# Attention and a state-space convolution in one kernel: half of x and all parameters transposed by DMA, zeroing by DMA, later bulk loads, and the accumulator copies on VectorE

## The chip, the core and the metric

The kernel runs on one core of one Trainium2 chip. The metric is the device time of one execution in microseconds, as the median of several executions. A profile is one further execution with the hardware profiler on; its times are counted from the first instruction, and its "span" is the time from the first instruction to the last.

## The reference

Two branches read the same input x (2048 rows of 448 numbers, bf16) and are mixed row by row with a gate g:

```python
x = A_x
g = _sigmoid((x * gate_w).sum(-1, keepdims=True))
a = _A_ref(x, A_wq, A_wk, A_wv, A_wo)
b = _B_ref(x, B_A_re, B_A_im, B_B_re, B_B_im, B_C_re, B_C_im, B_log_dt, B_Dskip)
return g * a + (1 - g) * b
```

Branch a is attention with 16 query heads of width 28 that share one key head and one value head:

```python
q = (lambda x, *d: x.transpose(*d))((x @ wq).reshape(B, S, H, Dh), 0, 2, 1, 3)
k = x @ wk
v = x @ wv
scores = jnp.einsum("bhqd,bkd->bhqk", q, k) * (Dh ** -0.5)
p = _softmax(scores, axis=-1)
o = jnp.einsum("bhqk,bkd->bhqd", p, v)
return (lambda x, *d: x.transpose(*d))(o, 0, 2, 1, 3).reshape(B, S, H * Dh) @ wo
```

Branch b is a causal convolution of every column of x with its own kernel of 2048 taps, plus x times Dskip. The taps come from 256 complex modes per column:

```python
logdA = dt * A
dB = dt * Bc
P = jnp.exp(logdA[:, :, None] * l[None, None, :])
K = jnp.einsum("dn,dnl,dn->dl", Cc, P, dB).real
```

The convolution is written with an FFT in the reference; the kernel computes it directly with matrix products.

## The kernel before

**Attention.** The work is cut into 16 blocks. Block i takes the 512 query rows of chunk i // 4 and the four heads of group i % 4. A block has 64 score tiles (16 key tiles by 4 heads) of 128 keys by 512 queries. Tiles are taken in sets of three and two in turn. For each set, TensorE computes the scores (L1181, "qk") into PSUM psS, ScalarE takes the exp of the whole set in one instruction (L1205) into a ring of 15 slots, expT, and TensorE multiplies four tiles at a time by the values (L1214, "PV") and adds into one PSUM bank, psB, called bank 6. One column of the values is 1, so the sum of the exps comes out in the same bank.

At the end of a block, `norm(i)` copies bank 6 to SBUF (the accumulator copy). Only then can the first PV of the next block overwrite the bank. The copy is ScalarE's for blocks 0 to 13 (L1074), VectorE's for block 14 (L1076), and the last block has an ending of its own. After the copy, GpSimd's queue carries three small DMAs that bring the sums into another layout and back (denT, R_scratch, rdenB), and VectorE multiplies by the reciprocal (L1088). Four blocks of one chunk then give the output rows (`outp`, `fold`).

Before block i + 2 the queries for it are projected (`qproj`): four matmuls (L816), a VectorE maximum of the magnitudes (L822), one matmul that subtracts a bound of the scores (L825), and a VectorE copy to bf16 (L828). The bound uses `kap`, the maximum over all keys, so no block can start before all four quarters of x have become keys.

**Convolution branch.** For groups of 32 columns, VectorE makes powers of the modes (`masters`) and tables of them (`tables`, L895 to L935). TensorE turns the tables into taps (`kgen`, L959), ScalarE evicts them (L972), and DMAs write them to a scratch tensor in HBM and read them back with shifted rows (T). TensorE then multiplies T by U, a layout of x with its rows in blocks of 64 (`conv`, L1015), VectorE scales (L1026), TensorE turns the result (L1037), and VectorE adds it into O (L1045), the output tile in SBUF. O and the padded rows of Wo must be zero before the first additions and products.

**The head.** Everything before the first exp of attention. x is loaded in four quarters of 512 rows (`loads`, xst). For each quarter (`prep_x`) TensorE transposes 16 squares (L565), ScalarE (L574) and VectorE (L576) each copy half of it to xT, TensorE makes the keys (L582), ScalarE evicts them (L588), and VectorE takes the maximum (L591). The columns of x are cut into four pieces of 112. In between, `prep_params` makes the seeds of the modes out of the six parameter tensors (448 x 256 each). Each is loaded with columns first (raw), transposed by TensorE (`trans`, L739), and multiplied on VectorE (L750, L753, L754, L756); ScalarE takes two sines (L757, L758) and two exps (L762, L764). VectorE also clears tiles (L450): U, Wq, Wk, Wo and O.

**What sets the order.** Nothing is ordered by hand. Every operation is recorded with an estimate of its length (ns), the keys it reads and writes, and a priority pr. The class `Prog` then plans: at each step it takes, over all engines, the operation that could start earliest, and among equals the one with the lower pr. It plans five queues: TensorE (pe), ScalarE (act), VectorE (dve), GpSimd (pool) and SP, which issues nearly all loads. Each engine carries out its planned list strictly in order, and waits on semaphores where the plan has a dependence. A DMA's planned cost comes from its row count and row size (`dma`, L140). A key that is read by one operation and written by a later one makes the later one wait for the earlier one's end, DMAs included. `fill` adds matmuls with a zero operand (L636, L640, L1187) where TensorE would have little to do.

The accumulator copy and the rule for the next PV in the code before:

```python
if i < 14:
    pg.op("act", lambda e: e.activation(av, self.psB.v(0, P, 0, [[1, 512]]), AF.Copy), 490, rd=[("b", 6)], wr=[ak, kb], pr=-1)
elif i == 14:
    pg.op("dve", lambda e: e.tensor_copy(av, self.psB.v(0, P, 0, [[1, 512]])), el(512), rd=[("b", 6)], wr=[ak, kb], pr=0)
...
o = pg.op("pe", mm, 230, rd=["va"] + [("e", t % RING) for t in ts], wr=[("b", 6)], pr=0.5, mode="c", st=4.54)
```

Of the kernel before, what the change touches and what calls it, by code (L numbers as in the profile page):

```python
# [11 lines left out]
P = 128  # L12
# [19 lines left out]
HALVES = (13,)  # L32
NTR = 5
# [47 lines left out]
class Prog:  # L81
# [52 lines left out]
    def dma(self, pairs, desc, slot, rd=(), wr=(), pr=0, eng="sp", slow=False, extra=0):  # L134
        kw = dict(allow_slow_non_contiguous=True) if slow else {}

        def fn(e):
            return [e.dma_start(o, i, **kw) for o, i in pairs]  # L138
        nd, size = desc
        o = self.op(eng, fn, nd * (30.0 + 0.03 * size if size < 1500 else 105.0 + 0.022 * size) / 16.0 * 1.1, rd, wr, pr)  # L140
        o.slot, o.ndma, o.extra = slot, len(pairs), extra
        prev = self.slots.get(slot)
        if prev is not None:
            o.deps[prev] = 1
        self.slots[slot] = o.i
        return o
# [210 lines left out]
class Kernel:  # L357
# [18 lines left out]
    def build(self):  # L376
        nc = self.nc
        with self.es:
# [5 lines left out]
            self.prep_params()  # L384
            self.prep_gate()
# [6 lines left out]
    def alloc(self):  # L392
# [26 lines left out]
        self.tslots = [(self.T, s * TW, ["tpdone", "rawdone"]) for s in range(NTR)]  # L419
# [26 lines left out]
    def consts(self):  # L446
# [13 lines left out]
        dm(self.Wq.v(0, P, 28, [[32, 64], [1, 4]]), 0.0, 300, ["Wq"])  # L460
# [22 lines left out]
        dm(V(self.Wo, 0, NT * D), 0.0, 810, ["Wo"], 5)  # L483
        for q in range(4):
            dm(V(self.O, q * 4 * D, 4 * D), 0.0, 800, [("O", q)], 5)

    def loads(self):
# [4 lines left out]
        def lx(q):  # L492
            pg.dma([(self.xst.v(0, P, q * 4 * D, [[1, 4 * D]]), dram(x, q * 4 * P * D, [[4 * D, P], [1, 4 * D]]))],
                   (128, 3584), f"x{q}", wr=[("xst", q)])
# [4 lines left out]
        def lraw(k):  # L499
            pg.dma([(raw.v(0, DT, k * 1024, [[1, 1024]]), dram(ins[names[k]], 0, [[1024, DT], [1, 1024]]))],  # L500
                   (112, 2048), f"raw{k}", wr=[("raw", k)])
# [3 lines left out]
        pg.dma([(self.dtb.v(0, P, 0, [[1, D]]), dram(ins["B_log_dt"], 0, [[0, P], [1, D]]))], (128, 896), "ldt", wr=["dt"], eng="act")  # L505
        lx(0)
        lraw(0)
        for k, (w, n) in enumerate((("A_wk", DH), ("A_wv", DH), ("gate_w", 1))):
            pg.dma([(wks.v(0, DT, 112 * k, [[n, 4], [1, n]]), dram(ins[w], 0, [[n, DT], [DT * n, 4], [1, n]]))],
                   (448, 2 * n), f"wk{k}", wr=[("wks", k)], eng="act", slow=True)  # L510
        for q in range(1, 4):
            lx(q)
        pg.dma([(wst.v(0, DT, 0, [[D, 4], [1, D]]), dram(ins["A_wq"], 0, [[D, DT], [DT * D, 4], [1, D]]))],
               (448, 896), "wq", wr=["wqs"])
        lraw(1)
        pg.op("dve", lambda e: e.tensor_copy(self.Wk.v(0, DT, 0, [[32, 16], [1, DH]]),
                                             wks.v(0, DT, 0, [[DH, 4], [0, 4], [1, DH]])), 300, rd=[("wks", 0)], wr=["Wk"], pr=-0.6)
        pg.op("dve", lambda e: e.tensor_copy(self.Wq.v(0, DT, 0, [[32, 64], [1, DH]]),
                                             wst.v(0, DT, 0, [[DH, 64], [1, DH]])), 620, rd=["wqs"], wr=["Wq"], pr=-0.5)
        pg.op("dve", lambda e: e.tensor_copy(self.Wv.v(0, DT, 0, [[32, 4], [1, DH]]), wks.v(0, DT, 112, [[DH, 4], [1, DH]])),  # L520
              180, rd=[("wks", 1)], wr=["Wv"], pr=0.1)
        pg.op("dve", lambda e: e.tensor_copy(self.Wv.v(0, DT, 28, [[32, 4]]), wks.v(0, DT, 224, [[1, 4]])),
              100, rd=[("wks", 2)], wr=["Wvg"], pr=0.1)
        rs = self.U.rs
        for k, (h, p0, b0) in enumerate(((1, 16, 15), (0, 0, 15), (1, 0, 31))):
            ap = bass.AP(tensor=self.U.h, offset=h * rs + p0 * D, ap=[[2 * rs, 64], [D, 16], [1, D]])
            pg.dma([(ap, dram(x, 64 * b0 * D, [[D, 64], [-64 * D, 16], [1, D]]))],
                   (1024, 896), f"u{k}", rd=["Uz"] if p0 else [], wr=[("U", k)], pr=0.5)
        for k in range(2, 6):
            lraw(k)  # L530
        pg.dma([(self.skt.v(32 * g + 31, 1, 0, [[8, 14], [1, 8]]), dram(ins["B_Dskip"], 8 * g, [[16 * D, 1], [32, 14], [1, 8]]))
                for g in range(4)], (112, 8), "sk", rd=["skt"], wr=["skt"], pr=1, slow=True)
        w = ins["A_wo"]
        pg.dma([(self.Wo.v(32 * r, DH, 0, [[D, 4], [1, D]]), dram(w, DH * r * D, [[D, DH], [4 * DH * D, 4], [1, D]]))
                for r in range(4)], (448, 896), "wo", rd=["Wo"], wr=["Wo"], pr=2)
        pg.dma([(dram(self.KP, KH + 1024, [[4 * KW, 112], [KW, 4], [1, 64]]), self.kstg.v(0, 112, 0, [[64, 4], [1, 64]]))],
               (448, 128), "pad", rd=[("kst", 0, 0), ("kst", 1, 0)], wr=["pad"], pr=3)
# [15 lines left out]
    def prep_x(self):  # L553
        pg = self.pg
        xst, xT, kT = self.xst, self.xT, self.kT
        sm = self.small
        for q in range(4):
            for hp in range(2):
# [3 lines left out]
                def mm(e, q=q, hp=hp, t=t, o=o):  # L562
                    for Tl in range(2):
                        for k in range(4):
                            r = e.matmul(t.v(0, DT, o + 512 * Tl + 128 * k, [[1, 128]]),  # L565
                                         xst.v(0, P, (4 * q + k) * D + (2 * hp + Tl) * DT, [[1, DT]]),
# [733 lines left out]
```

## Time and profile before

| What | Value |
|---|---|
| Median of three executions | 541.87 us (540.47 to 544.5) |
| The profiled execution | 540.75 us, span 539.0 us |
| ScalarE busy | 497.5 us (92%) |
| TensorE matmuls busy, fillers included | 486.4 us (90%) |
| VectorE busy | 449.5 us (83%) |
| GpSimd busy | 102.1 us (19%) |
| Exps of attention (L1205), 410 instructions | 470.6 us |
| Accumulator copies on ScalarE (L1074) | 14 |
| First exp of attention starts | 26.74 us |
| Last exp of attention ends | 527.7 us |

A row of the profile's order of time reads: start in us, length in us, engine, line of the kernel, operation, what it writes and reads with sizes, how many instructions the row merges, and in brackets how long the engine had been idle before it and what ended that. In the table of stages, each engine has its busy time and number of instructions within the stretch; PEclk is the clock granted to TensorE as a share of full speed. The chain of waits is followed back from the last instruction: at each step to what released it, or to the instruction before it on its engine.

### The profile page before, as it was taken

How to read it: one execution, taken by the hardware profiler on the slowest of the kernel's cores; microseconds unless marked ns; L12 is line 12 of the kernel's file. 1: busy time of each engine (PE TensorE's matmuls, PEld its weight loads, DVE VectorE, ACT ScalarE, POOL GpSimd, SP SyncE). 2: the span in 40 equal slices, each digit the busy share in tenths (PEclk: the TensorE clock that was granted, in tenths of full speed). 3: DMA queues.
4: the chain of work that ended last, by engine and by line, in shares of the span. 5: the costliest groups of instructions: out<-in, count | busy, mean ns of one | idle time of the engine just before them, and what ended most of it. 6: DMA issues, size and time to landing. Idle time of an engine off the chain costs nothing.

```text
span 539.0 us, 20180 instructions
## 1 busy us (share of the span) xinstructions
PE 486.4 (90%) x9186; PEld 249.5 (46%) x9186; DVE 449.5 (83%) x891; ACT 497.5 (92%) x458; POOL 102.1 (19%) x192
## 2 busy tenths in 40 slices
PE   7698999989999899888999898989999898999887
PEld 4442233235454555353555454553556355644434
DVE  7979999989999999899999999999999695331203
ACT  3799999998999999989999999999999796899992
POOL 2000002200431404012040430040042213220000
PEclk9989999998999999999999999999999796899998
DMA  8931100793398987979778989999859997999722
GB/s 235 283 121 47 37 21 7 251 347 116 118 376 300 329 358 284 351 259 386 296 240 363 327 273 348 400 351 367 343 191 356 353 380 287 348 344 392 261 88 71
DMA packets 39042, 142.89 MB, mean 265 GB/s; under 512 B 11240, under 2 KB 22032, under 8 KB 24620
## 3 DMA queue, kind: packets, MB, share of 16 engines
q1 hardware_dynamic: 28316, 135.30, 69.0%
q0 software_dynamic: 9104, 6.13, 4.4%
q8 instruction: 72, 1.18, 0.9%
q10 hardware_dynamic: 1536, 0.17, 0.3%
q14 instruction: 14, 0.11, 0.1%
HBM read 135.39 MB, written 5.74 MB: 262 GB/s over the span
## 4 chain that ended last, share of the span: by engine, by line
ACT 56%; PE 26%; DMA 8%; DVE 8%; issue 2%; ACTq 0%
ACT expT L1205 54%; PE psS L1181 7%; PE psB L1214 4%; PE psS L959 3%; PE psX L959 3%; DMA rdenB<-R_scratch 3%; PE psX L1015 3%; DMA denT<-acc 2%; DMA sz<-in_A_wv_dram 2%; PE psS L1015 2%; ACT acc L1074 1%; DMA R_scratch<-denT 1%; DVE msq L856 1%; DVE xT L576 1%; DVE tab L911 1%
## 5 line engine op out<-in xcount | busy, mean ns | idle before, releaser
L1205 ACT ACTIVATE expT<-psS 128x1536 bf16<-128x1536 f32 (+1 forms) x410 | 470.6, 1340 | 18.7 <-PE psS L1181 11.7
L1181 PE MATMUL psS<-qT,kT 32*128 32x512 bf16 x1024 | 164.3, 395 | 29.8 <-ACT expT L1205 22.3
L1214 PE MATMUL psB<-expT,vaug 128*32 128x512 bf16 x1024 | 105.1, 400 | 3.7 <-issue 3.2
L1181 PEld LDWEIGHTS psS<-qT,kT 32*128 32x128 bf16 x1024 | 39.5, 91 | 119.3 <-ACT expT L1205 97.3
L1187 PE MATMUL psB<-ident,zero 32*128 32x512 bf16 x190 | 74.9, 394 | 0.0
L911 DVE TENSOR_TENSOR tab<-tab,mbf 128x256 bf16<-128x256 bf16 (+5 forms) x75 | 69.6, 928 | 1.2
L1015 PE MATMUL psX<-T,U 128*18 128x128 bf16 (+7 forms) x1920 | 54.7, 243 | 4.2 <-issue 3.2
L1214 PEld LDWEIGHTS psB<-expT,vaug 128*32 128x32 bf16 x1024 | 26.4, 93 | 64.8 <-issue 62.8
L1015 PEld LDWEIGHTS psX<-T,U 128*18 128x18 bf16 (+7 forms) x1920 | 47.6, 161 | 15.1 <-issue 11.2
L640 PE MATMUL psB<-ident,zero 128*32 128x512 bf16 (+3 forms) x728 | 48.6, 336 | 0.0
L138 POOL DMA_DIRECT2D KP_scratch<-xT x64 | 34.4, 544 | 43.6 <-ACT xT L972 43.6
L138 POOL DMA_DIRECT2D KP_scratch<-kstg x63 | 34.1, 549 | 34.2 <-ACT kstg L972 32.5
L959 PE MATMUL psX<-tab 128*32 128x64 bf16 x960 | 39.7, 293 | 0.3 <-DVE tab L935 0.3
L913 DVE TENSOR_TENSOR tmp<-tab,mbf 128x256 bf16<-128x256 bf16 (+4 forms) x62 | 39.6, 638 | 0.0
L1015 PE MATMUL psS<-T,U 128*32 128x128 bf16 (+7 forms) x1344 | 39.3, 243 | 0.0
L138 POOL DMA_DIRECT2D denT<-acc x15 | 10.8, 717 | 146.8 <-ACT acc L1074 137.9
L1015 PEld LDWEIGHTS psS<-T,U 128*32 128x32 bf16 (+7 forms) x1344 | 34.0, 161 | 8.9 <-issue 6.9
L959 PE MATMUL psS<-tab 128*32 128x64 bf16 x832 | 35.3, 293 | 0.0
L138 POOL DMA_DIRECT2D R_scratch<-denT x15 | 8.6, 576 | 138.7 <-DVE denT L1082 59.2
L930 DVE TENSOR_TENSOR tab<-tab,tmp 128x2048 bf16<-128x2048 bf16 x28 | 33.5, 1219 | 0.2
L959 PEld LDWEIGHTS psX<-tab 128*32 128x32 bf16 x960 | 30.3, 138 | 6.7 <-issue 3.8
L959 PEld LDWEIGHTS psS<-tab 128*32 128x32 bf16 x832 | 26.4, 137 | 7.4 <-issue 5.4
(179 smaller groups left out, 599.1 us busy)
## 6 DMA issues: line engine op xcount, KB each, us to landing
T<-KP_scratch SPq DMA_DIRECT2D x102, 1072.0 KB, 11.0
xT<-KP_scratch SPq DMA_DIRECT2D x7, 1072.0 KB, 10.5
rdenB<-R_scratch POOLq DMA_DIRECT2D x15, 256.0 KB, 12.4
tab<-KP_scratch SPq DMA_DIRECT2D x3, 1072.0 KB, 8.8
U<-in_A_x_dram SPq DMA_DIRECT2D x3, 896.0 KB, 15.4
tab<-in_A_x_dram SPq DMA_DIRECT2D x4, 448.0 KB, 7.5
SZ_scratch<-tab SPq DMA_DIRECT2D x1, 1344.0 KB, 8.6
out_dram<-O SPq DMA_DIRECT2D x3, 448.0 KB, 3.8
```

Source lines behind the costliest of these rows:

```text
L138: return [e.dma_start(o, i, **kw) for o, i in pairs]
L576: pg.op("dve", lambda e, d=dst, s=src: e.tensor_copy(d, s), 1130, rd=[("b", b)], wr=[key], pr=-0.6)
L640: r = e.matmul(t.v(32 * j, 32, bo, [[1, 128 * m]]), self.zero.v(0, P, 0, [[1, 32]]), self.ident.v(0, P, 0, [[0, m], [1, P]]), start=not ac ...
L911: vo(lambda e, dst=dst, src=src, mr=mr: e.tensor_tensor(dst, src, mr, ALU.mult), 2 * n, done + mk(lv), kr + ki)
L913: vo(lambda e, src=src, mi=mi, w=w, n=n, tb=tb, to=to: e.tensor_tensor(tb.v(0, P, to, [[n, 2], [cw, w], [1, cw]]), src, mi, ALU.mult), 2 * ...
L930: vo(lambda e, h=h: e.tensor_tensor(tab.v(0, P, FM + 32 * h, [[64, 2], [EW, 32], [1, 32]]), tab.v(0, P, lo + 31 * EW + 64 * h, [[BLK, 2], ...
L959: r = e.matmul(G.v(32 * g, 32, 64 * jj, [[1, 64]]), tab.v(0, P, lo + comp * BLK + 32 + o, [[EW, 32]]), tab.v(0, P, fo, [[mo - fo, 2], [EW, ...
L1015: r = e.matmul(ps.v(32 * j, 32 - 2 * n, 128 * k, [[1, 128]]), self.U.v(0, P, 2 * n * D + 4 * gi + j, [[D, 32 - 2 * n]]), tb.v(0, P, to + j ...
L1181: r = e.matmul(self.psS.v(0, P, 512 * (bo + k), [[1, 512]]), kT.v(32 * h, 32, 128 * kt, [[1, 128]]), qT.v(32 * h, 32, 512 * (i % 2), [[1, ...
L1187: r = e.matmul(self.psB.v(0, P, 0, [[1, 512]]), self.zero.v(32 * h, 32, 0, [[1, P]]), self.ident.v(32 * h, 32, 0, [[0, 4], [1, P]]), start ...
L1205: pg.op("act", lambda e: e.activation(expT.v(0, P, 512 * es, [[1, n]]), self.psS.v(0, P, 512 * bo, [[1, n]]), AF.Exp, scale=SQ), 50 + n / ...
L1214: r = e.matmul(self.psB.v(32 * h, 32, 0, [[1, 512]]), vaug.v(0, P, 32 * kt, [[1, 32]]), expT.v(0, P, 512 * (t % RING), [[1, 512]]), start= ...
```

## The change

It has these parts.

- The accumulator copies of blocks 0 to 13 are made by VectorE (pr 0) instead of ScalarE (pr -1).
- Quarters 0 and 1 of x are transposed by DMA straight into xT; quarters 2 and 3 go the old way and come first. The four column pieces are now 128 wide (the fourth starts at column 320 and overlaps the third by 64 columns; the weights of the overlap are zero), so the copies of Wk, Wq, Wv and the gate's weights are split and get zeroed rows.
- The six parameter tensors are transposed by DMA; TensorE's transposes of them are gone, and the VectorE products read SBUF.
- Wo and O are zeroed by five DMAs from a zero tile, not by VectorE. These DMAs name ("mb", 10) as read, so the first writing of that key, the last level of the first `masters`, waits for them.
- The U, Dskip, Wo and pad transfers are recorded later (`late`), and Dskip and pad also wait for the seeds ("sqq"). The loads of the head get an order of their own (DP).
- wq is loaded in two pieces, the first with head group 0. The projections of the values are recorded tile by tile with a lower pr.
- The seeds of the first group are copied by VectorE instead of two DMAs. The last level of `masters` is written straight into the bf16 table.
- The planner's cost of a DMA row is lower for short rows.

The core of the diff:

```diff
+DP = dict(x2=-1.00, x3=-0.95, raw0=-0.90, x0=-0.85, raw1=-0.80, wq0=-0.75, x1=-0.70, wq1=-0.65)
...
-        o = self.op(eng, fn, nd * (30.0 + 0.03 * size if size < 1500 else 105.0 + 0.022 * size) / 16.0 * 1.1, rd, wr, pr)
+        o = self.op(eng, fn, nd * (12.0 + 0.036 * size if size < 1500 else 105.0 + 0.022 * size) / 16.0 * 1.1, rd, wr, pr)
...
+    def tdma(self, pairs, ns, slot, wr, pr):
+        o = self.dma(pairs, (1, 1), slot, (), wr, pr)
+        o.fn = lambda e: [e.dma_start_transpose(a, b) for a, b in pairs]
+        o.ns = ns
         return o
...
-        dm(V(self.Wo, 0, NT * D), 0.0, 810, ["Wo"], 5)
-        for q in range(4):
-            dm(V(self.O, q * 4 * D, 4 * D), 0.0, 800, [("O", q)], 5)
...
+            pg.tdma([(self.xT.v(0, P, 2048 * q, [[512, 3], [1, 512]]), dram(x, 512 * q * D, [[D, 512], [1, 384]])),
+                     (self.xT.v(0, P, 2048 * q + 1536, [[512, 1], [1, 512]]), dram(x, 512 * q * D + D - P, [[D, 512], [1, P]]))],
+                    2900, f"x{q}", wr=self.xk(q), pr=DP[f"x{q}"])
...
-            pg.dma([(raw.v(0, DT, k * 1024, [[1, 1024]]), dram(ins[names[k]], 0, [[1024, DT], [1, 1024]]))],
-                   (112, 2048), f"raw{k}", wr=[("raw", k)])
+            pg.tdma([(raw.v(0, P, k * 1024, [[D, 2], [1, D]]), dram(ins[names[k]], 0, [[NM, D], [1, NM]]))],
+                    1270, f"raw{k}", wr=[("raw", k)], pr=DP.get(f"raw{k}", 0))
...
-        for q in range(4):
-            for hp in range(2):
+        for q in (2, 3, 0, 1):
+            for hp in range(2) if q > 1 else ():
...
-        p0, k0 = trans(0, -0.4)
-        vt(tt(1), p0, dtp2, ALU.mult, [k0, "rd"], [K(1)], -0.4, unlock=p0)
+        vt(t(1), rw(0), dtp2, ALU.mult, [("raw", 0), "rd"], [K(1)], -0.65)
...
+    def late(self):
...
+        for k, (h, p0, b0) in enumerate(((1, 16, 15), (0, 0, 15), (1, 0, 31))):
...
+        for k, (b, n, keys, pr) in enumerate(((self.Wo, 14, ["Wo"], 1.9), *((Sub(self.O, 4 * D * q), 14, [("O", q)], 5 + q) for q in range(4)))):
+            pg.dma([(b.v(0, P, 0, [[P, n], [1, P]]), self.zero.v(0, P, 0, [[0, n], [1, P]]))], (P * n, 256), f"z{k}", rd=["zero", ("mb", 10)], wr=keys, pr=pr)
...
+            pg.op("dve", lambda e: e.tensor_copy(self.sz.v(0, P, 0, [[BW, 3], [1, w]]), self.seed.v(0, P, o, [[W2, 3], [1, w]])), 270,
+                  rd=["sz0", "sz1", "sq"], wr=["sre", "sim", "sqq"] + [("wks", k) for k in range(3)], pr=0.9)
...
+                if k == 10:
+                    dv(lambda e: e.scalar_tensor_tensor(last(1), f[0], 2.0, f[1], ALU.mult, ALU.mult), w, keys(9) + tp, [("mb", 10)])
+                    dv(lambda e: e.tensor_tensor(last(0), f[2], f[3], ALU.subtract), w, ["msq"] + tp, [("mb", 10)])
+                    continue
...
-        if i < 14:
+        if i < 0:
             pg.op("act", lambda e: e.activation(av, self.psB.v(0, P, 0, [[1, 512]]), AF.Copy), 490, rd=[("b", 6)], wr=[ak, kb], pr=-1)
-        elif i == 14:
+        elif i < 15:
             pg.op("dve", lambda e: e.tensor_copy(av, self.psB.v(0, P, 0, [[1, 512]])), el(512), rd=[("b", 6)], wr=[ak, kb], pr=0)
```

## The prediction, made before the result was known

> **What bounds the kernel now.** I first read the stages: the span was cut where the chain of waits and the order of time change character, and the busy time of each engine was taken in each cut. The cuts are: before the first exp, the first crowded stretch, the long body, the last stretch with convolution work, exps alone, and the end.
>
> ```profile
> core 0: us, PE busy (x) PEld busy (x) DVE busy (x) ACT busy (x) POOL busy (x), PEclk, DMA share, GB/s
> 0.00:26.74 26.74, 18.70 (x188) 11.29 (x188) 23.09 (x41) 14.79 (x16) 3.44 (x20) 0.97 0.94 261
> 26.74:42.50 15.76, 15.18 (x153) 6.12 (x156) 11.73 (x18) 13.99 (x13) 0.00 (x0) 0.84 0.30 104
> 42.50:420.00 377.50, 346.12 (x6915) 174.71 (x6907) 365.87 (x725) 369.96 (x339) 82.03 (x144) 0.99 0.74 268
> 420.00:471.50 51.50, 47.55 (x901) 27.59 (x901) 32.16 (x76) 41.51 (x39) 10.23 (x19) 0.80 0.94 341
> 471.50:527.70 56.20, 50.99 (x1002) 24.84 (x998) 12.06 (x23) 56.20 (x51) 6.44 (x11) 1.00 0.76 270
> 527.70:539.00 11.30, 7.88 (x40) 4.96 (x40) 4.62 (x11) 1.11 (x3) 0.00 (x0) 0.85 0.13 42
> ```
>
> ScalarE is the bound from 42.5 us on: 370.0 of 377.5 us busy, and 56.2 of 56.2 in the last stretch of exps. Only in 420 to 471.5 us does it idle for 10 us; there the granted clock is 0.80. VectorE is 97% busy in the body but 21% busy in the last 56 us, so its own total does not set the end. The first 26.7 us hold no attention exp at all.
>
> Next I read ScalarE's order of time around an accumulator copy, and the one block (the fifteenth) whose copy is already VectorE's.
>
> ```profile
> 59.55 0.78 ACT L1074 ACTIVATE acc<-psB 128x512 f32<-128x512 f32 x1
> 60.02 28.34 ACT L1205 ACTIVATE expT<-psS 128x1024 bf16<-128x1024 f32 x25
> ...
> 151.81 0.60 ACT L1074 ACTIVATE acc<-psB 128x512 f32<-128x512 f32 x1
> 152.30 4.64 ACT L1205 ACTIVATE expT<-psS 128x1536 bf16<-128x1536 f32 x4
> ```
>
> ```profile
> 499.71 0.69 DVE L1076 COPY acc<-psB 128x512 f32<-128x512 f32 x1 [2.83 <-PE psX L1015]
> ```
>
> A copy lasts 0.60 us, but the next exp begins 0.47 to 0.49 us after it began: 0.49 is what it takes from the exps. VectorE's copy is 0.69 us, and the exps around it run without a gap; but VectorE was idle there.
>
> Last, the chain of waits before the first exp, in order of time.
>
> ```profile
> 1.73 10.10 DMA sz<-in_A_wv_dram
> ...
> 14.17 1.14 DVE xT L576
> 15.31 1.00 DVE T L756
> 16.31 0.09 DVE expT L522
> 16.39 0.12 issue
> 16.51 0.81 DVE O L450
> 17.32 1.08 DVE xT L576
> 18.40 0.59 DVE small L591
> 18.98 1.13 DVE xT L576
> 20.11 0.53 DVE Wq L518
> 20.65 0.59 DVE small L591
> 21.24 1.00 DVE T L750
> ```
>
> From 11.8 to 24.8 us that chain is VectorE, almost without a break. Clearing O (0.81 us, and once more at 22.45) and the x copies (some 1.1 us each) stand in it. So VectorE's load sets the head, not arriving data.
>
> **What the Trainium skill says.** "ScalarE: Activation LUTs", section "What ACT_TABLE_LOAD costs", gives an ACTIVATE with immediates 186 ns + 0.833 N and an overlap of 93 ns between neighbours: 613 ns for 512 columns, 520 ns of stream. The trace agrees with the first (597 median) and has 0.47 to 0.50 for the second; I use 0.49. "VectorE: DVE Perf Modes", section "Why PSUM operands drop a tier", holds an fp32 PSUM source to the 1x rate; the 0.69 us above agrees, and in the chain such an instruction advances VectorE by 0.60. For a DMA transpose the trace has no row. "DMA: Bandwidth & Descriptors", section "Latency and other measured facts", has 261 GB/s for one with a non-contiguous middle dimension; the planner's costs in the diff (2.9 us for a quarter of x, 1.27 us for a parameter) are slower, 181 GB/s with the 64 columns of x that are read twice.
>
> **The change part by part.**
>
> *Accumulator copies.* 14 copies leave ScalarE. Twelve lie in the body, where it idles 2% of the time: 12 x 0.49 = 5.9 us gained. Two lie in 420 to 471.5 us, where TensorE at the lower clock holds the exps back anyway: 0 to 1.0 us. I take 6.0. VectorE gets 14 x 0.60 = 8.4 us. The new wait is TensorE's: the next block's first PV needs the accumulator bank, and behind that PV in TensorE's order stand the next scores, which ScalarE needs. The copy queues behind what VectorE has in hand, at most 2.28 us (the 4096-column products of L911 and L913), often 0.3 to 0.7. On ScalarE it also queued, behind an exp of 1.1 us. Bounds: nothing at all, and 1.4 us of idle ScalarE per boundary (priced below). I take nothing, because the planner orders scores ahead of that PV and one set of scores already in PSUM feeds ScalarE for another 1.1 us.
>
> *Head, VectorE.* Needed there before the first exp after the change: dt and its scaling 0.7, Wk 0.4, Wq for the first head group 0.3, the phase chain 1.08+0.62+1.08+1.08 = 3.9, two x copies 2.4, four key maxima 2.7, the second parameter 1.1, Wv and gate 0.5, kap and Wb 0.4, first q 1.4: 13.8 us. Starting at 7.2 us, as L729 does now, that gives 21.0 us. Gone from the stretch are two x copies (2.4) and two clears of O (1.6); three more clears stood before it.
>
> *Head, data.* SP now sends x2, x3, raw0, x0, raw1, wq0, x1 in this order. Today's first quarter of x is issued at 0.81 and used at 6.36: 5.5 us, of which 448 KB at the 283 GB/s of the page's second slice are 1.6, so 3.9 us are latency and company. Plain bytes ahead of x1's end (two quarters, a part of wq, small weights: 1.18 MB) take 4.2 us; the transposes by the planner's costs 2 x 2.9 + 2 x 1.27 = 8.3 us. Landing: 0.8 + 3.9 + 4.2 + 8.3 = 17.2 us. From there follow, by today's rows, the key projection 1.04, its eviction 0.69, the maximum 0.67, kap and Wb 0.41, L825 0.50, the q copy 0.69, the first scores 0.66 and some 0.5 of hand-overs: 5.2 us. First exp at **22.4 us** instead of 26.74, so 4.3 us gained. At the skill's 261 GB/s the data would be 2.6 us earlier (5.7 us instead of 8.3, an estimate from that page), and VectorE's 21.0 plus the last QK then decides, some 21.7. At half the planner's rate x1 lands at 25.5 and the first exp stands at 30.7, a loss of 4.0.
>
> *TensorE and ScalarE in the head.* 32 transposes of x and 48 of the parameters go (some 1.5 and 3.4 us of TensorE), two ScalarE x copies of 1.02. All stand beside VectorE's chain or x1's arrival: nothing more than counted. The parameter products keep their 1.08 us, reading SBUF instead of PSUM.
>
> *Zeroing by DMA, loads later.* 5 x 0.81 = 4.0 us leave VectorE, 1.6 counted above. Five DMAs of 1792 rows of 256 bytes come on SP. The U loads with 1024 rows kept SP for 10.10/3 = 3.4 us each; by rows that makes 5.9 us each, 29 us in all. Behind them wait Dskip, Wo, pad, the seed stores and the gate's round trip: SP is free near 50 us instead of 29. The first kernel taps are evicted at about 90 us, so this is hidden. One wait is new: the last level of the first masters writes what the zeroing names as read, so VectorE waits there for all five to land, about 53 us. That level stands at 59 us today: hidden, with little to spare.
>
> *Masters and seeds.* The last level is written straight into its table: 3 x 0.42 + 0.29 and 3 x 0.29 + 0.22 = 2.6 us less VectorE; two seed copies replace two DMAs, 0.6 more; the split weight copies and clears 0.9 more. VectorE's sum: +8.4 - 4.0 - 2.4 - 2.6 + 0.6 + 0.9 = +0.9 us. Since the last 56 us leave it 44 us idle: nothing.
>
> *Sum.* -6.0 - 4.3 = -10.3; I give back 0.3 for clears and copies that move into the crowded stretch after the first exp. 539.0 - 10.0 = 529.0 us of span. The profiled execution was 540.75 us and the median of three 541.87, so the prediction on the median is **531.9 us**.
>
> **The rivals.** (A) *Slow transposes.* At half the planner's rate the head costs 4.0 instead of giving 4.3: 541.87 - 6.0 + 4.0 = 539.9, no change. For it: no transposing DMA in the trace. Against it: two sources above the halved rate. (B) *Absorbed.* ScalarE idles 18 us after 40 us, 14 of them in stretches with a clock below 0.96; a new order of TensorE work can have more such stretches, and the freed 6 us turn into waits for scores: 541.87 - 4.3 = 537.6, no change. Against it: the body idles only 2%. (C) *Late copies*, the case on the slower side. VectorE is 97% busy, and a copy that finds it at L911 with L913 due next waits 2.3 to 4.6 us. TensorE then stands at the PV with the next scores behind it; one set of scores covers 1.1 us. Standing 2.5 us, ScalarE loses 1.4 us per boundary: 14 x 1.4 = 19.6, less the 6.0 and 4.3 gained: 541.87 + 9.3 = 551.2. It decides from 10.3/14 = 0.74 us per boundary. For it: nothing else fed by VectorE stands so directly before PV. Against it: q copies couple the two already, and TensorE's waits for them are about 1 us each in few places.
>
> **Numbers.** Forecast 0.60; (A) 0.12, (B) 0.14, (C) 0.10; faster still (fewer low-clock stretches, 522) 0.04. A measurement of this kernel can tell about 1% from no change, 5.4 us. Some of (A) and (B) still passes that: faster 0.70, same 0.18, slower 0.12. The low end takes the faster transposes (0.7), the two copies more (1.0) and 5 us less idling: 525. The high end passes (A) and (B) and stops inside (C): 543.5.
>
> **What would show it.** Right: the first exp near 22.4 us; ScalarE without 128x512 copies and its long runs of exps closed over the block boundaries; 14 VectorE copies of 0.69 us; an unchanged end of 11 us. Wrong: x1's transposes landing after 20 us, waits of PV for L1076 above 0.7 us a block, or ScalarE idle growing by more than 5 us between 42 and 470 us.

## The result and the profile after

The changed kernel takes 538.97 us (median of four executions) beside 542.46 us for the kernel before: a ratio of 0.9863, with a 95% interval of 0.9815 to 0.9912. In a later comparison, with 22 executions of it, the medians were 537.39 and 538.8 us and the ratio 0.9963 (0.9918 to 1.0008). So the gain is small, 0.4 to 1.4%, and the larger comparison can't tell it from none. Executions of one kernel differ by up to 3% (530.05 to 546.36 us for the changed kernel in the later comparison), the profiled one of the changed kernel is a long one (543.13 us; the other four took 534.52, 535.2, 535.42 and 542.73), and ratios leave the long ones out, so they are not the quotients of the medians.

The stages of the changed kernel, cut at its own first and last exp:

```profile
core 0: us, PE busy (x) PEld busy (x) DVE busy (x) ACT busy (x) POOL busy (x), PEclk, DMA share, GB/s
0.00:24.48 24.48, 17.46 (x151) 8.95 (x153) 20.70 (x46) 12.89 (x14) 3.44 (x20) 0.99 0.93 167
24.48:42.50 18.02, 17.17 (x168) 5.04 (x171) 17.03 (x41) 17.32 (x16) 0.00 (x0) 0.82 1.14 269
42.50:420.00 377.50, 348.79 (x6857) 173.10 (x6864) 360.76 (x696) 364.47 (x329) 78.11 (x137) 0.96 0.76 269
420.00:471.50 51.50, 46.41 (x815) 23.65 (x810) 35.54 (x82) 41.59 (x38) 13.99 (x26) 0.83 0.85 313
471.50:532.15 60.65, 55.05 (x1113) 29.23 (x1109) 13.87 (x30) 52.18 (x46) 5.98 (x10) 0.89 0.75 277
532.15:541.40 9.25, 6.34 (x40) 3.81 (x40) 4.44 (x11) 1.09 (x3) 0.00 (x0) 1.00 0.60 198
```

Against the kernel before, ScalarE is idle 13.0 us instead of 7.5 in the body, and 8.5 us instead of nothing between 471.5 us and the last exp; the granted clock there is 0.89, where it was 1.00. The groups of the exps, of PV and of the copy:

```profile
L1231 ACT ACTIVATE expT<-psS 128x1536 bf16<-128x1536 f32 (+1 forms) x410 | 470.6, 1338 | 34.4 <-PE psS L1207 28.3 <-remote 3.7 <-PE psB L1213 1.8
L1240 PE MATMUL psB<-expT,vaug 128*32 128x512 bf16 x1024 | 107.8, 412 | 0.9 <-issue 0.5 <-ACT expT L1231 0.2 <-DVE acc L1102 0.2
L1102 DVE COPY acc<-psB 128x512 f32<-128x512 f32 x15 | 10.3, 687 | 9.0 <-PE psB L1240 9.0
```

The exps cost what they did, 470.6 us. PV waits 0.2 us in all for VectorE's copy; it is the other way round, VectorE stands 9.0 us at the copy for the block's last PV. Around a block's end the exps now run on. First ScalarE's order of time, then VectorE's copy in it:

```profile
147.51 7.16 ACT L1231 ACTIVATE expT<-psS 128x1536 bf16<-128x1536 f32 x6
```

```profile
150.44 0.68 DVE L1102 COPY acc<-psB 128x512 f32<-128x512 f32 x1
```

The chain of waits before the first exp:

```profile
7.81 1.22 DVE xT L594
...
16.93 0.19 DVE Wq L541
17.15 1.09 DVE T L754
...
19.46 0.51 DVE Wq L541
19.97 0.99 DVE tab L754
20.97 0.60 DVE small L609
...
22.32 0.81 DVE tab L754
23.13 0.11 issue
23.23 0.69 DVE qT L844
```

It is VectorE still, from 7.81 to 23.9 us. In it stand the two products that make the seeds, "tab L754", which the forecast's list didn't have.

**The sum of the two profiled executions.** Call "stage" the time from the first exp's start to the last exp's end.

| | before | after | difference |
|---|---|---|---|
| until the first exp | 26.74 | 24.48 | -2.3 |
| ScalarE at work in the stage | 481.7 | 475.6 | -6.1 |
| ScalarE idle in the stage | 19.3 | 32.1 | +12.8 |
| from the last exp to the end | 11.3 | 9.3 | -2.0 |
| span | 539.0 | 541.4 | +2.4 |

The gain forecast for the copies is there, to a tenth. Idle time of ScalarE takes more than all of it back in this execution. But neither profile is of a typical execution: the one before is 1.7 us shorter than its median of 542.46 us, the one after 4.2 us longer than its 538.97. Between the medians lie -3.5 us; with the other three terms at -10.4 us, idle time grew by about 7 us (an estimate from this table and the medians). The experiments ask where that idle time comes from, and what else holds the end.

### The profile page after: what moved, and what is told of

It reads as the page before. It is cut to its first block, busy times and chain, and to the rows that moved or that the text cites. A ratio compares the mean times of both kernels' runs of the same rounds, so it can differ in the third digit from the quotient of the medians.

```text
span 541.4 us, 20063 instructions
## 1 busy us (share of the span) xinstructions
PE 491.2 (91%) x9119; PEld 243.8 (45%) x9139; DVE 452.3 (84%) x901; ACT 489.5 (90%) x442; POOL 101.5 (19%) x192
## 4 chain that ended last, share of the span: by engine, by line
ACT 55%; PE 26%; DVE 9%; DMA 7%; issue 2%; another core or an unknown queue 1%
ACT expT L1231 55%; PE psS L1207 8%; PE psB L1240 5%; DMA T<-KP_scratch 3%; PE psX L1041 2%; DMA denT<-acc 2%; PE psS L1041 2%; PE psS L985 2%; PE psX L985 1%; DMA tab<-in_A_x_dram 1%; PE psB L658 1%; DVE tab L937 1%; PE psX L1080 1%; PE psS L1166 0%
## 5 line engine op out<-in xcount | busy, mean ns | idle before, releaser
L1231 ACT ACTIVATE expT<-psS 128x1536 bf16<-128x1536 f32 (+1 forms) x410 | 470.6, 1338 | 34.4 <-PE psS L1207 28.3
L1207 PE MATMUL psS<-qT,kT 32*128 32x512 bf16 x1024 | 169.9, 407 | 27.7 <-ACT expT L1231 20.1
L1240 PE MATMUL psB<-expT,vaug 128*32 128x512 bf16 x1024 | 107.8, 412 | 0.9 <-issue 0.5
L1213 PE MATMUL psB<-ident,zero 32*128 32x512 bf16 x189 | 76.4, 404 | 0.0
L1240 PEld LDWEIGHTS psB<-expT,vaug 128*32 128x32 bf16 x1024 | 26.4, 94 | 63.6 <-issue 61.4
L1041 PE MATMUL psX<-T,U 128*32 128x128 bf16 (+7 forms) x1664 | 48.8, 244 | 4.8 <-issue 3.1
L658 PE MATMUL psB<-ident,zero 128*32 128x512 bf16 (+3 forms) x756 | 52.6, 348 | 0.0
L1041 PEld LDWEIGHTS psX<-T,U 128*20 128x20 bf16 (+7 forms) x1664 | 41.2, 162 | 16.9 <-issue 12.9
L1041 PE MATMUL psS<-T,U 128*26 128x128 bf16 (+7 forms) x1600 | 45.9, 241 | 1.2 <-issue 1.0
L1041 PEld LDWEIGHTS psS<-T,U 128*26 128x26 bf16 (+7 forms) x1600 | 40.4, 161 | 10.1 <-issue 7.6
L939 DVE TENSOR_TENSOR tab<-tab,mbf 128x4096 bf16<-128x4096 bf16 x13 | 29.7, 2282 | 0.0
## 6 DMA issues: line engine op xcount, KB each, us to landing
xT<-KP_scratch SPq DMA_DIRECT2D x7, 1072.0 KB, 10.4
```

Source lines behind the costliest of these rows:

```text
L658: r = e.matmul(t.v(32 * j, 32, bo, [[1, 128 * m]]), self.zero.v(0, P, 0, [[1, 32]]), self.ident.v(0, P, 0, [[0, m], [1, P]]), start=not ac ...
L939: vo(lambda e, src=src, mi=mi, w=w, n=n, tb=tb, to=to: e.tensor_tensor(tb.v(0, P, to, [[n, 2], [cw, w], [1, cw]]), src, mi, ALU.mult), 2 * ...
L1041: r = e.matmul(ps.v(32 * j, 32 - 2 * n, 128 * k, [[1, 128]]), self.U.v(0, P, 2 * n * D + 4 * gi + j, [[D, 32 - 2 * n]]), tb.v(0, P, to + j ...
L1207: r = e.matmul(self.psS.v(0, P, 512 * (bo + k), [[1, 512]]), kT.v(32 * h, 32, 128 * kt, [[1, 128]]), qT.v(32 * h, 32, 512 * (i % 2), [[1, ...
L1213: r = e.matmul(self.psB.v(0, P, 0, [[1, 512]]), self.zero.v(32 * h, 32, 0, [[1, P]]), self.ident.v(32 * h, 32, 0, [[0, 4], [1, P]]), start ...
L1231: pg.op("act", lambda e: e.activation(expT.v(0, P, 512 * es, [[1, n]]), self.psS.v(0, P, 512 * bo, [[1, n]]), AF.Exp, scale=SQ), 50 + n / ...
```

## The experiments

"Ratio" is against the kernel before on the same chip. "Last addition" is the start of the last addition of the convolution branch into O (L1045 before, L1071 after).

| kernel | median us | ratio (95%) | first exp | ScalarE work | ScalarE idle | last exp ends | last addition | span |
|---|---|---|---|---|---|---|---|---|
| before | – | 1 | 26.74 | 481.7 | 19.3 | 527.7 | 521.5 | 539.0 |
| changed | 538.97 | 0.9863 (0.9815–0.9912) | 24.48 | 475.6 | 32.1 | 532.2 | 533.3 | 541.4 |
| e1 copies only | 546.31 | 1.0183 (1.0122–1.0244) | 25.92 | 474.0 | 20.2 | 520.2 | 541.4 | 549.3 |
| e2 rest only | 549.19 | 1.0214 (1.0143–1.0285) | 24.48 | 481.9 | 27.7 | 534.1 | 516.4 | 543.4 |
| e3 changed again | 537.39 | 0.9963 (0.9918–1.0008) | 24.44 | 475.2 | 32.8 | 532.5 | 533.7 | 541.8 |
| e4 copy twice | 563.85 | 1.0440 (1.0358–1.0522) | 26.43 | 489.7 | 35.9 | 552.0 | 525.1 | 563.4 |
| e5 Wo after the store | 535.93 | 0.9916 (0.9880–0.9951) | 24.33 | 474.9 | 28.7 | 528.0 | 529.2 | 537.3 |
| e6 VectorE zeroes | 541.75 | 1.0081 (1.0046–1.0115) | 26.36 | 475.2 | 25.7 | 527.3 | 532.2 | 540.1 |
| e7 VectorE loaded | 554.22 | 1.0306 (1.0232–1.0379) | 26.29 | 482.1 | 23.2 | 531.7 | 539.6 | 547.5 |
| e8 seeds later | 537.82 | 1.0068 (1.0036–1.0099) | 23.21 | 474.8 | 22.9 | 520.9 | 528.4 | 536.3 |
| e9 store after the gate | 534.03 | 0.9924 (0.9891–0.9957) | 24.06 | 475.3 | 27.1 | 526.4 | 527.6 | 535.7 |
| e10 slack | 533.63 | 0.9932 (0.9904–0.9961) | 24.26 | 473.7 | 20.2 | 518.2 | 522.2 | 531.2 |
| e11 both | 529.24 | 0.9879 (0.9828–0.9931) | 24.55 | 474.1 | 16.3 | 514.9 | 518.8 | 528.3 |
| e12 half the copies | 557.11 | 1.0401 (1.0350–1.0452) | 24.46 | 479.0 | 40.4 | 543.9 | 528.8 | 555.1 |

**e1, the copies alone.** The kernel before with this edit:

```diff
-        if i < 14:
+        if i < 0:
...
-        elif i == 14:
+        elif i < 15:
```

> The kernel before with one edit: accumulator copies of blocks 0 to 13 on VectorE. Theory of the sum: 12 to 14 copies at 0.49 us leave a ScalarE that is the bound, so 5.9 to 6.9 us less, ratio 0.987 to 0.989. Rival (absorbed): the freed time turns into waits of ScalarE for scores, ratio 0.997 to 1.003. Rival (late copies): PV waits for the copy, ratio above 1.003, with waits of PV for VectorE's copy above 0.7 us a block.

The last exp ends 7.5 us earlier than before, but the kernel ends 10.3 us later in the profiles (e1's profiled execution took 551.05 us, its median is 546.31). None of the three expectations held: the kernel is slower, yet PV waits only 0.6 us in all for the copy. Its stages from 420 us on:

```profile
420.00:471.50 51.50, 47.57 (x998) 26.75 (x994) 43.66 (x94) 45.72 (x43) 14.40 (x26) 0.90 0.98 372
471.50:520.20 48.70, 43.71 (x901) 23.73 (x898) 10.94 (x22) 47.69 (x43) 5.86 (x11) 1.00 0.91 337
520.20:549.30 29.10, 16.00 (x331) 11.50 (x328) 8.26 (x18) 1.09 (x2) 0.70 (x1) 0.71 0.60 211
```

29 us are left after the last exp, where before had 11.3. The chain of waits at the end shows what fills them:

```profile
520.65 0.84 PE psS L1015 x30
521.49 13.72 DMA T<-KP_scratch
535.25 1.11 PE psX L1015 x29
...
540.99 0.40 PE psX L1037 x16
541.41 0.43 DVE O L1045
541.89 0.36 PE psS L1146
```

There are two chains. One is the exps. The other is the convolution branch: tables on VectorE, taps, their way through HBM (the 13.72 us), the convolution, the addition into O. In e1 the second chain ends the kernel, and 7.9 us pass from the start of its last addition to the end, as they do in e6, e7 and e8. In the kernel before, VectorE waits for that addition's input and makes it at 521.5 us:

```profile
521.46 0.42 DVE L1045 TENSOR_TENSOR O<-O,psS 128x256 bf16<-128x256 bf16 x1 [2.82 <-PE psS L1037]
```

With those 7.9 us that makes 529.4, so some 9.6 us of slack (an estimate). Moving 8.4 us of copies to VectorE moved the addition by 19.9 us.

**e2, the rest without the copies.** The changed kernel with the copies of blocks 0 to 13 back on ScalarE:

```diff
-        if i < 0:
+        if i < 14:
...
-        elif i < 15:
+        elif i == 14:
```

> The changed kernel with the accumulator copies back on ScalarE. Theory of the sum: only the head's gain is left, first exp near 24.5 us, so 1 to 3 us less than before, ratio 0.994 to 0.998. Rival (absorbed copies): the whole gain stays, ratio 0.986.

Alone, the rest is slower too, which neither expectation allowed for. ScalarE idles 8.4 us more than before, 4.0 us of it in one wait near 54 us that e5 and e9 look into; that is not the whole loss, since the profiled execution took 545.11 us where the median is 549.19. But the last addition comes 5 us earlier (521.5 to 516.4), some 19 us ahead of what the end allows.

With the copies, in the changed kernel, the last addition stands at 533.3 us. That is not the branch's own time. VectorE makes it straight after the copies for the last PV, without waiting for its input, whose last matmul (L1063) had ended at 531.74. ScalarE runs its last exps without a pause up to 532.15 us:

```profile
509.75 22.40 ACT L1231 ACTIVATE expT<-psS 128x1536 bf16<-128x1536 f32 x20 [0.15 <-PE psS L1207]
```

```profile
532.66 0.76 DVE L1121 COPY acc<-psB 128x256 f32<-128x256 f32 x2 [2.27 <-PE psB L1240]
533.33 0.41 DVE L1071 TENSOR_TENSOR O<-O,psS 128x256 bf16<-128x256 bf16 x1
```

So the exps set the end of the changed kernel, and in e3, e5 and e9 too the last addition starts 1.2 us after the last exp has ended. Neither half of the change gains; together they are 0.4 to 1.4% faster.

**e3, the changed kernel again.** No edit, on the chip of e1, e2 and e4.

> The changed kernel once more, for a profile of it beside the others on one chip. Ratio 0.986 as before; span near 533 us, the first exp at 24.5 us.

The ratio is closer to 1 than expected. The profile has the same sum as the first one (first exp 24.44, work 475.2, idle 32.8, last addition 533.7), and it too lies above its median, by 6.1 us.

**e4, each copy made twice on ScalarE.** The kernel before with

```diff
-            pg.op("act", lambda e: e.activation(av, self.psB.v(0, P, 0, [[1, 512]]), AF.Copy), 490, rd=[("b", 6)], wr=[ak, kb], pr=-1)
+            for _ in range(2):
+                pg.op("act", lambda e: e.activation(av, self.psB.v(0, P, 0, [[1, 512]]), AF.Copy), 490, rd=[("b", 6)], wr=[ak, kb], pr=-1)
```

> The kernel before, with each of the 14 ScalarE copies made twice in a row (the second writes the same values again). If ScalarE is the bound in the body, each further copy costs 0.49 us: 14 x 0.49 = 6.9 us more, ratio 1.011 to 1.013. If a copy is absorbed in idle time, less than 3 us more, ratio below 1.005.

ScalarE's work grows by 8.0 us, 0.57 for each of 14 copies, somewhat more than the 0.49 of the forecast: a copy is not absorbed. The time grows by more, because idle time grows by 16.6. Two waits are as long as all of it (ScalarE's order of time):

```profile
288.71 0.59 ACT L972 ACTIVATE xT<-psX 128x504 bf16<-128x504 f32 x1 [5.51 <-DVE xT L969]
300.73 1.23 ACT L1075 ACTIVATE acc<-psB 128x512 f32<-128x512 f32 x2 [11.43 <-DVE onT L1089]
```

The second is a copy that waits 11.4 us until VectorE has multiplied out of the buffer it writes: acc has two buffers, and VectorE's product of two blocks earlier was late.

**e5, Wo later.** Near 54 us ScalarE, VectorE and TensorE of the changed kernel all wait at once (called a stand below). Its line of ScalarE:

```profile
57.87 2.37 ACT L1231 ACTIVATE expT<-psS 128x1024 bf16<-128x1024 f32 x2 [3.67 <-remote]
```

At that time the loads of Wo, the gate's write to HBM (512 rows of four bytes) and the store of the seeds are on their way. This edit holds Wo back:

```diff
-                 for r in range(4)], (448, 896), "wo", rd=["Wo"], wr=["Wo"], pr=2)
+                 for r in range(4)], (448, 896), "wo", rd=["Wo", "SW"], wr=["Wo"], pr=2)
```

> The changed kernel; the four Wo loads also wait for the second seed store (SW_scratch) to land. In the changed kernel ScalarE, VectorE and TensorE stand together for 3.7 to 4.0 us at 53 us, while packets of that store and of Wo take 3 to 9 us each. Theory (the Wo loads collide with the store): the stand vanishes, ScalarE idles 4 us less, 3 to 4 us less than the changed kernel, ratio to before 0.980 to 0.991. Rival (the store collides with the gate's 4-byte writes, which stay beside it): the stand stays at 50 to 58 us, time as the changed kernel.

A stand of 3.23 us stayed at 53.9 us. Wo isn't the cause. (In the changed kernel the longest packets took 8.7 us in the store and 2.9 us in Wo, but half of them took less than 0.1 us.)

**e6, zeroing by VectorE again.** The changed kernel with the clears of Wo and O put back and the five zeroing DMAs left out:

```diff
+        dm(V(self.Wo, 0, NT * D), 0.0, 810, ["Wo"], 5)
+        for q in range(4):
+            dm(V(self.O, q * 4 * D, 4 * D), 0.0, 800, [("O", q)], 5)
```

> The changed kernel with Wo and O cleared by VectorE again, no zeroing DMAs. Theory: SP is free 15 us earlier, the Wo loads leave before the seed store, the stand at 53 us vanishes (4 us), VectorE's 4 us of clears are hidden or cost the head up to 1.6 us: 2 to 4 us less than the changed kernel. Rival (zeroing by DMA is a gain of 4 us of VectorE): 2 to 5 us more than the changed kernel, the first exp after 25.5 us.

The rival held: the median is 541.75 us, and the first exp comes 1.9 us later than in the changed kernel, which is what zeroing by DMA is worth in the head. SP comes to the gate's write (35.02 us) and the store (38.37) earlier, and the stand near 54 us is gone. The store here is issued 3.35 us behind the write, while SP issues the read that waits for the write only at 46.54; no engine stands for it. So the two being under way together isn't enough for a stand.

**e7, VectorE loaded.** The kernel before with the multiplication by the reciprocal made twice for 15 blocks, some 9 us:

```diff
-            pg.op("dve", lambda e: e.tensor_tensor(ov, av, self.rdenB.v(0, P, 0, [[1, 512]]), ALU.mult),
-                  el(512), rd=[ak, kb, "rd", "onw"], wr=[("on", on(i))], pr=2, slk=SLK[1])
+            for _ in range(2):
+                pg.op("dve", lambda e: e.tensor_tensor(ov, av, self.rdenB.v(0, P, 0, [[1, 512]]), ALU.mult),
+                      el(512), rd=[ak, kb, "rd", "onw"], wr=[("on", on(i))], pr=2, slk=SLK[1])
```

> The kernel before with VectorE's product at the end of each block (L1088) made twice, the same values: 15 x 0.60 = 9 us more of VectorE, nothing more for ScalarE. Theory (VectorE's load delays the convolution branch, which ends just before the exps): the last addition into O moves from 521 us to 530 to 545, and the kernel takes 4 to 16 us more, ratio 1.008 to 1.03. Rival (the prediction's step: VectorE has 44 us to spare at the end): ratio 0.998 to 1.002, the last addition stays within 3 us.

ScalarE's work is unchanged (482.1), but the last addition moves from 521.5 to 539.6 us and the kernel ends 7.9 us after it. The exps end 4.0 us later as well, and the last turn stands in TensorE's list behind the first output products, so the branch alone doesn't set this end; but its last convolution matmul now ends at 534.8 us instead of 517.9, behind the last exp. Load on VectorE is not free, although VectorE is nearly idle in the last 50 us: by then the tables have been made, too late (the last one at 475.5 us instead of 463.5).

**e8, seeds later.** The changed kernel, with the seeds and two products made to wait for the first queries:

```diff
-        vt(zc(0), tc(5), tc(4), ALU.mult, [K(5), K(4)], ["sz0"], 1)
+        vt(zc(0), tc(5), tc(4), ALU.mult, [K(5), K(4), ("q", 0)], ["sz0"], 1)
...
-        vt(t(6), rw(2), dtb, ALU.mult, [("raw", 2), "dt"], [K(6), ("wqs", 0), ("wqs", 1)], 3)
-        vt(t(7), rw(3), dtb, ALU.mult, [("raw", 3), "dt"], [K(7)], 3)
+        vt(t(6), rw(2), dtb, ALU.mult, [("raw", 2), "dt", ("q", 0)], [K(6), ("wqs", 0), ("wqs", 1)], 3)
+        vt(t(7), rw(3), dtb, ALU.mult, [("raw", 3), "dt", ("q", 0)], [K(7)], 3)
```

> The changed kernel; four VectorE products of the parameters (two seeds, two B products) also wait for the first block's queries. Theory (VectorE's list sets the head): the first exp moves from 24.5 us to 22.5 to 23.5, and the kernel takes 1 to 2 us less than the changed one if the rest of the plan keeps its shape. Rival (x1's transposes set the head): the first exp stays at 24.2 us or later.

The first exp comes at 23.21 us, 1.3 us earlier. No gain follows (ratio 1.0068 beside e3's 0.9963): the exps end at 520.9 us, and the last addition at 528.4 sets the end.

**e9, the store after the gate.** The changed kernel with

```diff
-               (256, 1792), "sst2", rd=["sw0", "sw1"], wr=["SW", "seeds2"], pr=5)
+               (256, 1792), "sst2", rd=["sw0", "sw1", "GT"], wr=["SW", "seeds2"], pr=5)
```

> The changed kernel, only that the store of the seeds to SW_scratch is issued after the gate's write of 512 four-byte rows has landed. Theory 1 (the two transfers beside each other cause the stand of all engines near 53 us): no ScalarE idle above 1.5 us between 50 and 58 us, ScalarE idle in the stage of exps 3 to 4 us less than the changed kernel's 32 us, 0.993 of the changed kernel. Theory 2 (the gate's four-byte write alone causes it, or something that neither transfer is): a stand of 3 to 4 us stays within 3 us of where it was, time within 0.4% of the changed kernel's.

The stand is gone. ScalarE's order of time at that place:

```profile
44.33 18.33 ACT L1231 ACTIVATE expT<-psS 128x1536 bf16<-128x1536 f32 x16
```

The gate's write still lands 10.3 us after its issue, but the store, now issued at 57.36, lands in 4.7 us where it took 13.0. ScalarE idles 5.0 us less than in the changed kernel's profile. The other runs agree. In the seven profiles with a stand (the changed kernel, e2, e3, e5, e8, e10 and e12; 3.2 to 4.9 us) the store is issued 0.66 to 1.06 us behind the write; in the seven without one (the kernel before, e1, e4, e6, e7, e9 and e11) it is issued 3.35 us (e6) or more than 10 us behind it. So the stand comes with a store close behind the four-byte write. Whether in e6 the distance or the other traffic decides, and through what three engines are stopped at once ("remote"), the traces don't show. In time e9 and the changed kernel can't be told apart: the ratio is 0.9924 beside e3's 0.9963, and the intervals overlap.

**e10, more slack for the reciprocal.** In the profiles of the changed kernel, e3, e5 and e9 a stretch of low clock (the granted clock is 0.5) begins between 340 and 348 us. The waits of e3 from 343 to 352 us show a chain:

```profile
DVE denT L1108 <- DMA denT<-acc: 3.3, 1, 3.3
PEld psX L1041 <- DVE O L1089: 3.1, 1, 3.1
PE psX L1041 <- DVE O L1089: 2.8, 1, 2.8
ACT expT L1231 <- PE psB L1213: 2.6, 1, 2.6
```

VectorE's list has come to the reciprocal before its DMA has landed; what TensorE needs next stands behind it; the exp behind that. The edit tells the planner to put the reciprocal later:

```diff
-SLK = (4000, 4000, 800)
+SLK = (9000, 4000, 800)
```

> The changed kernel, only that the planner puts the reciprocal of the sums (L1108) 5 us later behind its DMA. Theory 1 (VectorE's wait of 3.3 us for that DMA near 345 us stops TensorE and begins a low-clock stretch of 14 to 20 us): VectorE's waits for denT above 1 us gone, no low-clock stretch above 7 us between 330 and 375 us, ScalarE idle in the stage 4 to 6 us less than the changed kernel's 32 us, 0.99 of the changed kernel. Theory 2 (low-clock stretches come with the body's load and move elsewhere): low-clock time in all within 10 us of the changed kernel's 63 to 69 us, time within 0.4%.

No wait of VectorE for that DMA is left, no low-clock stretch lies between 67 and 463 us, and low-clock time in all falls from 68.3 us (e3: 61.4) to 30.7; in e11, with the same edit, it is 23.9, again with none near 345 us. The exps of the stretch are one run:

```profile
339.63 21.99 ACT L1231 ACTIVATE expT<-psS 128x1536 bf16<-128x1536 f32 x19
```

The exps end 14 us earlier than in the changed kernel's profile. The end comes 10 us earlier: it is now 13.0 us behind the last exp, because matmuls of the convolution branch (last addition 522.2) stand in the chain between the last PV and the output rows. These 10 us are not all the edit's: the profile of the changed kernel lies 4.2 us above its median and this one 0.7 us below. Over 22 executions each the ratio is 0.9932 beside e3's 0.9963, some 2 us, with overlapping intervals.

**e11, both.** The edits of e9 and e10.

> The changed kernel with both edits, the store after the gate's write and the reciprocal 5 us later. If the two stands are what stops the exps, ScalarE idle in the stage is 7 to 10 us less than the changed kernel's 32 us; but the convolution branch (last addition into O at 533.5 us, 8 us before the end) then sets the end unless it moves too, so 0.985 of the changed kernel at best and 0.995 if only the exps come earlier.

ScalarE's idle time is 16.3 us, half of the changed kernel's, and the stages from the body to the end are:

```profile
42.50:420.00 377.50, 347.58 (x6880) 175.04 (x6886) 364.17 (x700) 368.85 (x333) 79.78 (x141) 0.99 0.75 270
420.00:471.50 51.50, 46.65 (x977) 28.17 (x978) 36.79 (x86) 44.96 (x41) 11.85 (x22) 0.97 0.95 350
471.50:514.93 43.43, 40.19 (x881) 21.37 (x876) 9.45 (x19) 43.15 (x39) 5.95 (x10) 1.00 0.88 324
514.93:528.30 13.37, 9.24 (x105) 6.28 (x94) 5.68 (x13) 1.09 (x3) 0.00 (x0) 0.87 0.42 138
```

With a median of 529.24 us (526.67 to 531.82) it has the lowest median of all, 1.2% below the kernel before; the profile's span is 13 us below the changed kernel's. Its interval and that of e3 touch, so the ratio alone doesn't place it ahead of the changed kernel. As in e10, convolution work (L1041, L1052) stands in the chain behind the last exp: 13.4 us follow that exp instead of 9.3, and of the 17.2 us by which the exps end earlier than in the changed kernel's profile, 13.1 are had.

**e12, half the copies.** The changed kernel with

```diff
-        if i < 0:
+        if i < 14 and i % 2:
```

> The changed kernel with the copies of the odd blocks 1 to 13 (7 of 14) back on ScalarE. Two chains (exps and convolution): ScalarE's work in the stage 475.6 + 7 x 0.5 = 479 us, the last addition into O starts 8 to 9 us earlier than the changed kernel's 533.5, and the exps alone set the end, so that the time is 1.00 to 1.01 of the changed kernel's, and 8 us or more lie between the last addition's end and the end of the kernel. One chain (only ScalarE's work counts): the same 3.5 us more, but the last addition stays at 530 us or later.

A miss of more than 3%. The work is as expected (479.0). The last addition is at 528.8 us, 4.5 us before the changed kernel's and not 8 to 9; but that expectation took the 533.5 us for the branch's own time, which it isn't (e2). But ScalarE's idle time is 8.3 us more than in the changed kernel, and one wait makes most of it:

```profile
417.05 0.61 ACT L1100 ACTIVATE acc<-psB 128x512 f32<-128x512 f32 x1 [7.12 <-DVE onT L1114]
420.89 1.02 ACT L1231 ACTIVATE expT<-psS 128x1024 bf16<-128x1024 f32 x1 [3.23 <-PE psB L1240]
```

It is e4's wait again: a copy on ScalarE that needs a buffer which VectorE hasn't read out yet (it reads it at 416.33), and after it an exp that waits for the PV queued behind the copy. With the copy on VectorE, both stand on one engine in order, and ScalarE doesn't stand there. The time isn't a simple mean of the two kernels.

## Why the prediction was right in direction, and where it failed

The forecast was 531.9 us, and 538.97 was measured, inside the range of 525 to 543.5. The direction rests on a step that held (the copies), one that held in part (the head) and on a gain that was mostly given back: of 10.0 us forecast, 3.5 came in the first comparison and 1.4 in the later one, whose interval includes no change. So that the direction came out is in part luck. The sum had no term for new idle time of ScalarE, and that is what it lacked most (below, rival B).

**Accumulator copies, "I take 6.0": right.** ScalarE's work fell by 6.1 us here, by 7.7 in e1 and by 6.3 from e2 to the changed kernel, and rose by 8.0 where the copies were doubled; the agreement to a tenth is chance. The wait that rival C priced didn't come: PV waited 0.2 us in all for the copies.

**"VectorE's sum ... nothing": this step failed.** "Since the last 56 us leave it 44 us idle" looked at VectorE's total against the exps' end. The runs show a second chain through VectorE that has its deadline earlier: the tables must be ready before the taps go through HBM and the convolution. It had some 9.6 us of slack before. Loads of 8.4 us (e1) and 9 us (e7) moved its last addition by 19.9 and 18.1 us, to behind the end of the exps, and the two kernels are 1.8 and 3.1% slower than the kernel before. In the changed kernel itself this chain doesn't set the end (e2), so the step's reason was wrong, but it is not what took the gain back there. Why the branch has room there is not shown: the other parts alone bring its last addition 5 us forward, but with the copies its last table is made at 475.7 us, later than in e1 (474.4), and yet its last turn has ended at 531.74, where e1's last addition comes at 541.4.

**Head, "First exp at 22.4 us": right in kind, too large.** It came at 24.48, a gain of 2.3 us and not 4.3. The data term was good: the last transpose of x1 landed at 16.48 us (17.2 forecast). Rival A is out: the pair of x1 landed 4.7 us after its first issue (2.80 us of it issuing), 0.52 MB at 112 GB/s with latency included. By this measure the 261 GB/s that "DMA: Bandwidth & Descriptors", section "Latency and other measured facts", of the Trainium skill gives were not reached, and needn't have been. The term mis-sized is VectorE's "13.8 us": from 7.3 us to the end of the q copy it took 16.6. Missing were the two products that make the seeds (1.8 us of the chain), pieces of Wq (0.8) and smaller weight pieces. e8, which moved them out of the way, put the first exp at 23.21.

**Zeroing.** SP was done with it at 40.25 us, in 12.5 us of issuing for O and 2.5 for Wo, and not the 29 us estimated by rows; VectorE's new wait for ("mb", 10) was hidden, as forecast. What the step didn't see: by moving SP's list it brought the gate's write (issued at 31.21 us before, 47.44 after) and the store of the seeds (44.28 and 48.50) to within 1.06 us of each other, and a stand of 3.7 us followed. In e9, which parts them, it is gone.

**Rival B, "Absorbed", names what took the gain back.** ScalarE's idle time, for which the sum had nothing, grew by 12.8 us in the profiles and by about 7 between the medians (the estimate above). The prediction's own sign of being wrong, more than 5 us of it between 42 and 470 us, came true by a little (from 17.5 to 22.9 us between 42.5 and 471.5). Two edits show parts of it: without the stand at 54 us the idle time is 5.0 us less (e9), without the wait for the small DMA near 345 us 11.9 us less (e10, where most low-clock stretches after 471.5 us are gone too, which the edit alone doesn't explain). With both edits the idle time is 16.3 us, below that of the kernel before. These are differences of single profiles, and those of the changed kernel and e3 lie 4.2 and 6.1 us above their medians. That the two waits are gone is shown; how many microseconds each cost is not: by the ratios e9 and e10 are 0.4 and 0.3% faster than e3, and e11 0.8% (some 4.5 us). The 2.0 us gained at the end, where the forecast had "an unchanged end of 11 us", have no explanation here. The rival's own reason, a new order of TensorE work with more low-clock stretches, is right as far as a stop of TensorE comes ahead of the stretch that was taken apart; for the others that wasn't tried.

**Left open.** Why a load on VectorE delays the convolution branch by about twice its size isn't settled. Part of it is VectorE's list: the last table is made 10.9 us later in e1 and 12.0 us later in e7. The other 9.0 and 6.1 us arise between the last table and the last addition (58.0 us before, 67.0 in e1, 64.1 in e7). In e1 the last load of T starts only when matmuls of the branch have ended at 521.49; what delays those was not tried.

## What to carry to other kernels

List every chain that ends near the end, with its slack, before an engine's idle time is called free: an engine that is idle in the last stage may have had an earlier deadline. When a chain's end is read from an instruction on an engine that works in order, see whether the instruction waited for its input or only for its turn. When a copy is moved between engines, look at who must free its target, since a copy in the bound engine's list lets a late reader of another engine stop it. When loads are moved later, look at which transfers they now meet, and test a new stand by shifting one of them. Before two profiles are subtracted, see how far each lies from its kernel's median.

## What the runs showed of the hardware

- The time of an execution goes with its granted clock. Over the 22 executions of e3 the correlation is -0.93 and 0.01 of clock goes with 3.7 us; over 59 executions of the kernel before, -0.89 and 4.1 us.
- In the changed kernel, e3, e5 and e9 near 345 us a stop of TensorE (1.7 to 2.8 us) comes just ahead of a stretch of 10 to 21 us at low clock, in which a score matmul lasts 0.60 us and not 0.39; in e10 and e11 the stop and the stretch are gone. Over all 14 profiles, between 42 us and the last exp, 33 of the 36 stops of TensorE longer than 1.7 us have a low-clock stretch that begins in them or within 3.5 us after them; 17 of the 77 stretches have no stop above 1 us beside them.
- A write of 512 four-byte rows to HBM lands 9.7 to 11.9 us after its issue (e11, e9, after); a store of 448 KB issued 0.66 to 1.06 us behind it lands after 10.6 to 13.0 us (seven profiles), and after 4.7 to 5.2 us when it is issued once the write has landed (e9, e11).
- On SP, issuing the DMA transpose of a parameter (448 x 256) took 1.2 to 1.7 us, and it landed 3.0 to 7.6 us after its issue.
